# Waiting for the output stores in two steps at the end of SyncE's program

## The chip, the cores and the metric

The kernel runs on one core of one Trainium2 chip. The metric is the device time of an execution in microseconds (us); lower is better. Each kernel was run several times, in rounds that alternate with the kernel before on the same chip. A second number belongs to each execution, the **span**: from the first to the last instruction of the program itself. The timed execution is longer than the span, because closing code runs after the program's last instruction.

A ratio below is the mean time of one kernel's fast runs over that of the other's of the same rounds, so it is not quite the ratio of the medians that are quoted beside it. A run counts as slow when it is more than 1.5% above the fastest of the same kernel; slow runs are left out of the ratios, but not of the medians. Spans of single runs are on record to 0.1 us, so a difference of time and span is good to 0.05 us.

## The reference

For x of 2048 x 448 (bf16), the result is x plus two branches of its layer norm: a linear attention with 16 heads and a softmax feature map, and a dense SiLU block.

```python
xn = _layernorm(x, axis=-1)
return x + _A_ref(xn, A_wqkv, A_w_phi, A_wo) + _B_ref(xn, B_w1, B_w2)
```

Only the way the result leaves the chip matters for what follows: 16 tiles of 128 rows are written from on-chip memory to HBM as they are finished.

## The kernel before

The kernel schedules its own operations and then emits one instruction stream for each engine. A finished tile is added up by VectorE and stored by a DMA. Stores are numbered, and number n counts on the semaphore of slot n mod 4. The last tile is split in two halves: ScalarE issues the first half's store, SyncE the second's.

```python
NOS = 4
out_sems = [sem(f"s_out{i}") for i in range(NOS)]
# ... cut ...
def out_ev(t, ob, addend, cs):
    res = x_sb[:, t, :]
    P.op("dve", ..., lambda e: e.tensor_tensor(res[:, cs], ob, addend[:, cs], ALU.add), ..., name="out_ev")
    P.dma(lambda e: e.dma_start(out=rows_of(out, t, t + 1)[:, 0, cs], in_=res[:, cs]), ..., name="out_dma",
          out_slot=ob_cnt[0] % NOS, eng="sp" if cs.start else "act")
    ob_cnt[0] += 1
```

There are 17 stores, so the slots take 5, 4, 4 and 4 of them. Each store adds 16 to its slot's semaphore. SyncE issues most of the kernel's loads and transpositions as well; its program ends with waits for all slots, so that nothing ends before the output has landed:

```python
def emit_engine(ename, eng):
    waited = {}
    for oid in order[ename]:
        # ... cut: the waits that this operation needs ...
        ins = o.fn(eng)
        if o.is_dma:
            ins.then_inc(o.dma_sem, 16)
        # ... cut ...
    if ename == "sp":
        for i in range(NOS):
            if out_cnt[i] > 0:
                eng.wait_ge(out_sems[i], 16 * out_cnt[i])
```

A wait call is not yet an instruction. In the compiled program two calls share one wait instruction, and they are paired from the inside of the list to the outside. The four calls 0, 1, 2, 3 become two instructions: (slot 2 full, slot 1 full), then (slot 3 full, slot 0 full). The store that lands last is the 17th, on slot 0.

The softmax here doesn't subtract the row's maximum and nothing guards it: scores larger than these inputs give would overflow.

## Time and profile before

| | before |
|---|---|
| time, median of the first 3 runs | 149.02 us (148.81 to 149.06) |
| span of the profiled run | 147.6 us |
| TensorE busy | 143.4 us, 97% |
| SyncE instructions | 79 |
| last compute instruction ends | 145.98 us |
| last store lands | 147.61 us |

The lines that carry the table are shown and read in the prediction. In them, SPq is SyncE's own queue of instructions, L1119 is line 1119 of the kernel, and 28/218/407 are the least, median and greatest duration in ns. One more table: the same kernel cut at the 501st matmul and at the end of TensorE's work. Its columns are stretch and length, then the busy times of TensorE matmul, weight load, VectorE, ScalarE and GpSimd with instruction counts, then clock, DMA share and GB/s.

```profile
0.00:46.60 46.60, 44.45 (x500) 25.72 (x502) 32.78 (x85) 32.58 (x48) 25.10 (x56) 1.00 0.83 199
46.60:145.50 98.90, 98.90 (x1076) 54.03 (x1070) 57.80 (x111) 39.24 (x44) 48.94 (x37) 1.00 0.44 82
145.50:147.70 2.20, 0.04 (x1) 0.00 (x0) 0.47 (x2) 0.00 (x0) 0.00 (x0) 1.00 0.28 80
```

TensorE waits 2 us in all in the first stretch, never in the second, and is done in the third.

### The profile page before, as it was taken

Reading aid. Unit: us, or ns where it says so; the run is one execution under the profiler, and the core shown is the slowest. Engines: PE = TensorE matmul, PEld = TensorE weight load, DVE = VectorE, ACT = ScalarE, POOL = GpSimd, SP = SyncE. Lnnn points to the kernel's source line nnn. Section 1 sums busy time; section 2 is a strip of 40 time slices with the busy share of each in tenths; the row PEclk is TensorE's granted clock in tenths of the full one; section 3 lists DMA queues with packets and bytes.
Section 4 is the critical chain, followed back from the end, with each engine's and each line's share of the span. In section 5 each row is a group of like instructions: output and inputs, shape, how many; then the busy total and the mean of one; then the engine's idle time right before and its main releaser. Section 6 shows DMA issues by size and latency. Waiting matters only on the chain.

```text
span 147.6 us, 3735 instructions
## 1 busy us (share of the span) xinstructions
PE 143.4 (97%) x1572; PEld 79.7 (54%) x1572; DVE 91.1 (62%) x196; ACT 71.8 (49%) x92; POOL 74.0 (50%) x92
## 2 busy tenths in 40 slices
PE   7989999999999999999999999999999999999994
PEld 7884444544544557655444455555555465555473
DVE  2958997190799889207993018969701958252383
ACT  4657675759994988998655597080000000000000
POOL 8618566501099999996999600983940000000000
PEclk9999999999999999999999999999999999999999
DMA  4999964899920000000387391079676925542154
GB/s 109 331 355 247 295 119 70 154 134 301 334 61 0 0 0 4 4 4 0 41 172 147 77 141 36 0 148 119 127 142 134 232 84 98 107 38 39 34 174 137
DMA packets 44496, 17.53 MB, mean 119 GB/s; under 512 B 37040, under 2 KB 44096, under 8 KB 44480
## 3 DMA queue, kind: packets, MB, share of 16 engines
q1 hardware_dynamic: 41648, 15.10, 50.5%
q10 hardware_dynamic: 2704, 2.17, 4.4%
q8 instruction: 12, 0.20, 0.6%
q0 software_dynamic: 128, 0.03, 0.1%
q14 instruction: 4, 0.03, 0.1%
HBM read 6.57 MB, written 1.84 MB: 57 GB/s over the span
## 4 chain that ended last, share of the span: by engine, by line
PE 92%; DMA 4%; SPq 1%; DVE 1%; issue 1%; ACT 0%
PE psum L482 91%; DMA phT<-in_B_w_dram 4%; SPq L516 1%; DVE x_sb L896 1%; DVE Wqk L636 0%; PE psum L497 0%; ACT last_lo L502 0%; ACT last_hi L502 0%
## 5 line engine op out<-in xcount | busy, mean ns | idle before, releaser
L482 PE MATMUL psum<-xnT,phT 64*128 64x512 bf16 (+1 forms) x428 | 45.6, 350 | 0.9 <-DMA phT<-in_B_w_dram 0.4
L482 PE MATMUL psum<-w_sb,hT 128*128 128x448 bf16 (+1 forms) x238 | 45.4, 341 | 0.0
L814 POOL TENSOR_TENSOR RA<-Ek_sb,Rec 128x896 bf16<-128x896 bf16 x16 | 27.0, 1721 | 13.1 <-DVE Rec L779 10.2
L502 ACT ACTIVATE hT<-psum 128x1024 bf16<-128x1024 f32 x28 | 27.3, 1024 | 12.8 <-PE psum L482 12.8
L778 DVE TENSOR_REDUCE Rec<-Ek_sb 128x32 f32<-128x896 bf16 (+1 forms) x20 | 24.4, 1252 | 14.4 <-POOL Ek_sb L509 7.5
L482 PEld LDWEIGHTS psum<-w_sb,hT 128*128 128x128 bf16 x238 | 22.2, 98 | 18.7 <-issue 1.1
L482 PEld LDWEIGHTS psum<-xnT,phT 64*128 64x128 bf16 (+1 forms) x428 | 21.0, 95 | 20.9 <-PE psum L482 0.6
L502 ACT ACTIVATE Ek_sb<-psum 128x864 bf16<-128x864 f32 x24 | 20.1, 910 | 7.1 <-POOL RA L814 4.4
L482 PE MATMUL psum<-Wqk,xnT 64*128 64x432 bf16 x224 | 23.4, 343 | 0.1
L874 DVE TENSOR_SCALAR den<-psum 128x16 f32<-128x16 f32 x16 | 2.3, 156 | 23.3 <-PE psum L482 23.3
L482 PEld LDWEIGHTS psum<-Wqk,xnT 64*128 64x128 bf16 x224 | 10.5, 94 | 10.1 <-issue 0.8
L788 POOL TENSOR_TENSOR Ek_sb<-Ek_sb,Rec 128x896 bf16<-128x896 bf16 x8 | 13.3, 1700 | 5.1 <-DVE Rec L779 5.1
L788 POOL TENSOR_TENSOR phT<-phT,Rec 128x896 bf16<-128x896 bf16 x8 | 13.3, 1702 | 0.0
L482 PE MATMUL psum<-wv,xnT 64*128 64x448 bf16 x112 | 12.9, 349 | 0.0
L643 DVE BATCH_NORM_STATS2 st<-x_sb 128x6 f32<-128x448 bf16 x16 | 9.6, 603 | 2.9 <-DMA x_sb<-in_A_x_dram 2.9
L482 PE MATMUL psum<-wo_sb,vaug 128*128 128x448 bf16 (+1 forms) x51 | 10.8, 342 | 0.0
L896 DVE TENSOR_TENSOR x_sb<-psum,x_sb 128x448 bf16<-128x448 f32 (+1 forms) x14 | 7.5, 584 | 5.0 <-PE psum L482 5.0
L881 DVE TENSOR_TENSOR vaug<-psum,rden 128x448 bf16<-128x448 f32 x16 | 9.8, 623 | 0.4
L658 DVE TENSOR_SCALAR RA<-x_sb,mv,rstd 128x384 bf16<-128x384 bf16 (+4 forms) x29 | 8.9, 346 | 1.3 <-POOL rstd L654 1.1
L779 DVE RECIPROCAL Rec<-Rec 128x32 f32<-128x32 f32 (+1 forms) x24 | 8.8, 396 | 0.2
L778 DVE TENSOR_REDUCE Rec<-phT 128x64 f32<-128x1792 bf16 x4 | 8.0, 2004 | 0.6 <-ACT phT L502 0.6
L482 PEld LDWEIGHTS psum<-wv,xnT 64*128 64x128 bf16 x112 | 5.5, 94 | 5.2
(59 smaller groups left out, 110.6 us busy)
## 6 DMA issues: line engine op xcount, KB each, us to landing
out_dram<-x_sb ACTq DMA_DIRECT2D x15, 112.0 KB, 1.7
w_sb<-in_B_w_dram SPq DMA_DIRECT2D x1, 1568.0 KB, 8.1
x_sb<-in_A_x_dram SPq DMA_DIRECT2D x3, 448.0 KB, 6.2
wo_sb<-in_A_wo_dram SPq DMA_DIRECT2D x2, 336.0 KB, 7.6
phT<-in_B_w_dram SPq DMA_DIRECT2D x1, 576.0 KB, 7.2
phT<-in_B_w_dram SPq DMA_DIRECT2D x2, 256.0 KB, 4.5
phT<-in_B_w_dram ACTq DMA_DIRECT2D x1, 384.0 KB, 4.8
wv<-in_A_wqkv_dram SPq DMA_DIRECT2D x1, 336.0 KB, 7.3
```

Source lines behind the costliest of these rows:

```text
L482: r = e.matmul(dst, lhsT, rhs, start=st, stop=sp, skip_group_check=True)
L502: P.op("act", d_act(n), lambda e: e.activation(dst, src, func, scale=scale), reads=[src], writes=[dst], table=table, name=name, **keys)
L516: P.dma(lambda e: e.dma_start(out=dst, in_=src), n / 280.0, writes=[dst], name=name, eng=eng, lat=lat)
L643: P.op("dve", 590, lambda e: e.bn_stats(st6[:, t, :], xs), reads=[xs], writes=[st6[:, t, :]], name=f"bnst{t}", okeys_w=["ln"])
L658: P.op("dve", dur, lambda e: e.tensor_scalar(dst, x_sb[:, t, c0:c1], mv[:, t, 0:1], rstd[:, t:t + 1], ALU.subtract, ALU.mult), reads=[xs, ...
L778: P.op("dve", 50 + 967 * n, lambda e: e.tensor_reduce(R2, E4, AXL.X, ALU.add), reads=[E4], writes=[R2], name="Ssum")
L779: P.op("dve", 135 + 210 * n, lambda e: e.reciprocal(R2, R2), reads=[R2], writes=[R2], name="Rrec")
L788: P.op("pool", 1700, lambda e: e.tensor_tensor(E3, E3, Rk[:, :, None].broadcast_to([128, 32, DH]), ALU.mult), reads=[E3, Rk], writes=[E3], ...
L814: P.op("pool", 1700, lambda e: e.tensor_tensor(dst, Eq, Rq.rearrange("p (c j) -> p c j", c=CC)[:, :, :, None].broadcast_to([128, CC, 4, DH ...
L874: P.op("dve", 190, lambda e: e.tensor_scalar(den[:, uq, :], U3[:, :, DH], EPS_DEN, None, ALU.add), reads=[U3[:, :, DH]], writes=[den[:, uq ...
L881: P.op("dve", 620, lambda e: e.tensor_tensor(o3, U3[:, :, 0:DH], rden[:, uq, :, None].broadcast_to([128, H, DH]), ALU.mult), reads=[U3[:, ...
L896: P.op("dve", d_dve(cs.stop - cs.start), lambda e: e.tensor_tensor(res[:, cs], ob, addend[:, cs], ALU.add), reads=[ob, addend[:, cs]], wri ...
```

## The change

The intent can be read from the code: SyncE first waits for all stores but the last of each slot, then for the last, so that most of the waiting work is done before the last store lands. The lower counts prove nothing that the full counts do not, so the result is the same.

```diff
             if ename == "sp":
-                for i in range(NOS):
-                    if out_cnt[i] > 0:
-                        eng.wait_ge(out_sems[i], 16 * out_cnt[i])
+                for back in (1, 0):
+                    for i in range(NOS):
+                        if out_cnt[i] > back:
+                            eng.wait_ge(out_sems[i], 16 * (out_cnt[i] - back))
```

Eight calls in place of four make four wait instructions in place of two. The rest of every engine's program is unchanged.

## The prediction

> **What bounds the kernel now.** I read the page first, then the stretch table of the end, the chain, the timeline of the last microseconds, and last the one source line that the change touches.
>
> ```profile
> span 147.6 us, 3735 instructions
> PE 143.4 (97%) x1572; PEld 79.7 (54%) x1572; DVE 91.1 (62%) x196; ACT 71.8 (49%) x92; POOL 74.0 (50%) x92
> q14 instruction: 4, 0.03, 0.1%
> PE 92%; DMA 4%; SPq 1%; DVE 1%; issue 1%; ACT 0%
> ```
>
> TensorE is busy for 97% of the span and makes up 92% of the chain that ended last. SyncE does not appear among the engines of the first part: its program only issues transfers and waits. So nothing that SyncE does in the first 146 us matters unless it delays a transfer that TensorE needs, and the change leaves that part of its program alone. The third line counts instruction packets on one queue; it is used further down.
>
> The stretch table shows where TensorE stops:
>
> ```profile
> 140.00:146.00 6.00, 5.54 (x48) 4.08 (x46) 4.54 (x9) 0.00 (x0) 0.00 (x0) 1.00 0.50 172
> 146.00:147.70 1.70, 0.00 (x0) 0.00 (x0) 0.00 (x0) 0.00 (x0) 0.00 (x0) 1.00 0.25 68
> ```
>
> The columns after the length are the busy times of TensorE matmul, weight load, VectorE, ScalarE and GpSimd, with instruction counts, then clock, DMA share and GB/s. From 146.0 us on, no compute engine does anything. The last 1.6 us are a store and a wait. The timeline and the view of the store and of the waiting line say what happens in them:
>
> ```profile
> 145.20 0.78 DVE L896 TENSOR_TENSOR x_sb<-psum,x_sb 128x224 bf16<-128x224 f32 x2 [0.76 <-PE psum L482]
> 145.62 0.34 ACTq L898 DMA_DIRECT2D out_dram<-x_sb  x1
> 146.07 0.37 SPq L898 DMA_DIRECT2D out_dram<-x_sb  x1
> ```
> ```profile
> L1119 SPq EVENT_SEMAPHORE  x2: 28/218/407, 146.5 to 147.2; - x2
> ```
> ```profile
> SPq L1119 <- DMA out_dram<-x_sb: 1.1, 1, 1.1
> ```
> ```profile
> out_dram<-x_sb SPq DMA_DIRECT2D x1, 56.0 KB, 1.5
> ```
>
> VectorE ends the two half tiles at 145.20 + 0.78 = 145.98. ScalarE issues the first half's store at 145.62, SyncE the second half's at 146.07 and is free at 146.44. Then SyncE runs the waiting line, L1119. The source has four wait calls there, one for each output slot, but the row says x2: two wait instructions, so two semaphores go into each. Their durations are 28 and 407 ns (least and most) and they start at 146.5 and 147.2. The second therefore ends at 147.2 + 0.41 = 147.6, the end of the span. The SyncE wait view puts 1.1 us on a landing store, and the issue table has the last store landing 1.5 us after 146.07, at 147.6. So **the landing of the last store ends the program**, and the number of waits in front of it does not show.
>
> **Exact times from the trace's semaphore records**, since the views round. Slots 1 and 2 reached their full counts at 145.65 and 146.16, before the first wait instruction ran (146.48). Slot 3 (the ScalarE half) was full at 147.210; the last wait instruction is recorded from 147.226. Slot 0 (the SyncE half) was full at 147.611; that instruction ends at 147.633. Of the 407 ns, some 385 are the wait for slot 0.
>
> **What the Trainium skill says.**
> "Perfetto Trace Analysis", section "Sequencer-only Instruction (DRAIN, etc)": the reported start of such an instruction comes when all its semaphores are satisfied, so waiting is not in its duration. This trace agrees for the first semaphore (start 16 ns after slot 3 was full) and differs for the second, whose 385 ns are inside the 407.
> "DMA: Bandwidth & Descriptors", section "Why a DMA increments its semaphore by 16 and not by 1": only a full count proves that a transfer landed; a lower count with two transfers in flight can be filled by either. The added waits use a lower count, so they prove nothing, but the full-count waits stay behind them and keep the program right. The trace has exactly 16 landing records for each store.
> "Runtime: NRT & Kernel Launch", section "Instruction fetch mechanics": instructions are fetched in blocks of 16 KiB, 256 instructions, ahead of use, and crossing a block is "mostly hidden". The trace has 12 packets of 16 KiB on queue 8, as that says, but queue 14's are 8 KiB each (0.03 MB over 4), which would be 128 instructions. No run here shows yet whether a crossing costs SyncE anything.
>
> **The change, part by part.** Stores go round four slots; there are 15 + 1 on ScalarE and 1 on SyncE, 17, so the slots hold 5, 4, 4 and 4. The new first pass waits for all but the last of each slot: counts 64, 48, 48, 48. That is four more wait calls, which at two to an instruction are **two more instructions**. Nothing is removed or moved; the old four calls stay last.
>
> What the new ones wait for: by the semaphore records, slot 0 had its 64 at 145.09, slot 1 its 48 at 142.75, slot 2 at 143.26, slot 3 at 144.56. SyncE gets to them at 146.48. The youngest is 1.39 us old, so neither waits. Each then costs what a satisfied two-semaphore wait costs: 28 ns busy, and 58 to 65 ns from start to start of the next instruction where SyncE runs one directly ahead of another instruction (at 75.03, 90.55 and 124.48 us). Two cost 2 x 0.06 = 0.12 us.
>
> What that lies beside: the first old wait instruction is done at 146.51 and the second can't pass its first semaphore before 147.21, so there are 0.70 us of slack. 0.12 of 0.70 is used. On the path to the end: **0.00 us**. The span should stay at 147.6. If the time follows the span, the prediction is 149.02.
>
> **The rivals.**
> (1) *A later last wait.* If the pairing changes so that slot 0's full count is no longer in the last instruction, the others run after it landed: one to three satisfied instructions of 0.06 us, +0.06 to +0.17 us. For it: the compiler already reorders (it paired slots 2 and 1, then 3 and 0). Against: the pair with slot 0 was put last before. Time: up to 149.2.
> (2) *The instruction fetch.* The timed 149.02 is 1.4 us more than the span, so something after the last wait is in it. In the trace's packet records, an 8 KiB instruction packet of queue 14 starts at 148.72, 1.09 us after the last wait. SyncE's own store at 146.07 had its first packet at 146.93, 0.86 us later, and its first load, issued at 0.80, at 1.84, 1.04 us later. So a fetch that starts at 148.72 may have been asked for at about 147.7 to 147.9, just after SyncE's last instruction. It is plausibly SyncE's: VectorE accounts for two of the four inside the span (22.5 and 122.2 us, when it had started 61 and 189 instructions, 128 apart), and ScalarE and GpSimd can hold the two at 41.2 and 44.0. If two more instructions move SyncE's block boundary to the near side of its wait, the request falls into time that is waited out anyway. What it then saves is at most the packet's 0.46 us, and some of that may have been beside the closing work of other engines: -0.1 to -0.4, 148.6 to 148.9. For it: the position. Against: the skill calls the crossing mostly hidden, and nothing in this trace shows an engine stalled by it.
> (3) *The fetch gets in the way.* The same shift puts an 8 KiB packet near the final store. A packet asked for at 146.55 would start at about 147.5, after the store's last data packet (147.26). Little is at risk: at most a part of 0.46 us on one of 16 engines, 149.0 to 149.4.
>
> **Range and chances.** I give the null 60%, rival 2 30% at about -0.25, the other two 10% at about +0.15. The weighted shift is -0.075 + 0.015 = -0.06 us; I set 148.95. Repeats of the kernel before spread from 148.81 to 149.06. Eight times in ten it should be within 148.55 to 149.25: the lower end is most of rival 2, the upper is rival 1 or a slow repeat. A change of 2% would be 2.98 us, more than the whole 1.6 us from the last compute to the end, and no part of this change touches the TensorE chain. So 0.98 for within 2%, and 0.01 on either side for an unforeseen effect.
>
> **What would show it.** The waiting line should list four instructions, three of about 28 ns and one of some 400, from 146.5 to 147.2, and the span should stay at 147.6 within 0.3. SyncE's wait for the last store should stay at about 1.0 us. If rival 1 holds, the longest of them is not the last and the span grows by 0.06 to 0.17. If rival 2 holds, the span is unchanged, the time falls, and the page counts a fifth packet on queue 14 because it now starts before the span ends. The prediction is wrong if TensorE's busy time or the timeline before 146 us differs by more than repeats do: then the program's length acts on something that no view here shows.

## The result, and the profile after

| | before | after |
|---|---|---|
| time, median of 6 runs | 149.14 us (148.81 to 149.31) | 149.42 us (149.23 to 149.94) |
| ratio, 95% interval | 1 | 1.0025 (1.0005 to 1.0045) |
| span of the profiled run | 147.6 us | 148.0 us |
| timed less span, every run with a span | 1.73 to 1.85 us | 1.23 to 1.30 us |

By the 2% rule this is the same time. It lies above the predicted range all the same, and the last two rows say that something real happened: the span of the profiled run went up, and the time outside the span went down by 0.5 us in every run.

The page of the changed kernel differs in its first line only by what was added, and TensorE's work is what it was:

```profile
span 148.0 us, 3737 instructions
PE 143.1 (97%) x1572; PEld 79.9 (54%) x1572; DVE 91.0 (61%) x196; ACT 71.6 (48%) x92; POOL 74.0 (50%) x92
q14 instruction: 4, 0.03, 0.1%
```

The stretch table of the changed kernel, cut at the same instructions as the one before:

```profile
0.00:46.30 46.30, 44.18 (x500) 25.79 (x502) 32.69 (x85) 32.33 (x48) 25.09 (x56) 1.00 0.83 200
46.30:145.20 98.90, 98.90 (x1076) 54.07 (x1070) 57.82 (x111) 39.23 (x44) 48.94 (x37) 1.00 0.43 82
145.20:148.00 2.80, 0.04 (x1) 0.00 (x0) 0.47 (x2) 0.00 (x0) 0.00 (x0) 1.00 0.21 62
```

The middle stretch has the same length and the same 1076 matmuls. The first is 0.3 us shorter in this execution, which is chance, as shown below. The last is longer by 0.6 us. Its timeline and its waiting line, which was L1119 and is L1120 now:

```profile
144.89 0.77 DVE L896 TENSOR_TENSOR x_sb<-psum,x_sb 128x224 bf16<-128x224 f32 x2 [0.76 <-PE psum L482]
145.76 0.37 SPq L898 DMA_DIRECT2D out_dram<-x_sb  x1
```
```profile
L1120 SPq EVENT_SEMAPHORE  x4: 28/28/28, 147.3 to 148.0; - x4
```
```profile
out_dram<-x_sb SPq DMA_DIRECT2D x1, 56.0 KB, 1.5
```

SyncE is free at 145.76 + 0.37 = 146.13, and its store lands 1.5 us after issue, at 147.3, as before. The four wait instructions were expected to start from 146.1 on. **All four start at 147.3 or later**, each takes 28 ns, and the last starts at 148.0: nothing was waited out ahead of the landing. The trace's records give the exact order (the slots are from the trace, the counts from the compiled program):

| start, us | waits for (compiled program) | |
|---|---|---|
| 147.319 | slot 0 full (80), slot 3 at 48 | slot 0 became full at 147.303 |
| 147.389 | slot 1 full, slot 2 at 48 | |
| 147.877 | slot 2 full, slot 1 at 48 | 0.46 us after the one ahead of it ended |
| 147.956 | slot 3 full, slot 0 at 64 | |

So two things stand out. The call for the last landing, fifth in the list of eight, was paired with the fourth and came **first**. And between the second and third instruction SyncE pauses for 0.46 us, where the others follow each other in 0.07 to 0.08 us from start to start. In the kernel before the pause isn't in the span. But its closing code started late: its barrier's first record after the landing came 0.685 us after the landing, of which only 0.02 were the end of the last wait instruction. In the changed kernel that record came 0.811 us after the landing. The clear difference of the tails is thus 0.126 us, in two parts of opposite sign.

An instruction packet of 8 KiB on queue 14 starts 1.091 us after the end of SyncE's 79th instruction in both traces (at 148.724 and 148.508 us). In the kernel before the 79th instruction is the last wait; in the changed one it is the second of the four.

### The profile page after: what moved, and what is told of

The parts are those of the page before. It is cut to its first block, busy times and chain, and to the rows that moved or that the text cites. A ratio compares the mean times of both kernels' runs of the same rounds, so it can differ in the third digit from the quotient of the medians.

```text
span 148.0 us, 3737 instructions
## 1 busy us (share of the span) xinstructions
PE 143.1 (97%) x1572; PEld 79.9 (54%) x1572; DVE 91.0 (61%) x196; ACT 71.6 (48%) x92; POOL 74.0 (50%) x92
## 4 chain that ended last, share of the span: by engine, by line
PE 90%; DMA 3%; ACT 2%; DVE 1%; SPq 1%; issue 0%
PE psum L482 90%; DMA phT<-in_B_w_dram 3%; ACT hT L502 1%; SPq L516 1%; DVE Wqk L636 1%; DVE x_sb L896 1%; PE psum L497 0%; ACT last_hi L502 0%; ACT last_lo L502 0%
```

## The experiments

Two theories and a null were set against each other. **Theory O** (order and crossing): SyncE pauses for some 0.45 to 0.55 us after its 79th instruction, where it goes into the next block of its program, and each satisfied instruction behind the one that waits for the last landing adds 0.06 us. **Theory L** (length): a longer program is slower, or, turned round, any longer program is free of the pause. **Theory N**: chance.

Three measures are used: the clock with its ratio, the timed execution less span (in each run), and the tail, from the last landing to the first record of the closing barrier after it, in the one trace of each kernel.

### The changed kernel again

No edit.

> The changed kernel once more, for a narrower interval and a second trace. Theory O (order and block crossing: the last-landing store's wait stands first of four, and SyncE stalls some 0.4 to 0.5 us after its 79th instruction, in the old kernel after its last wait, here between the second and third of the four): first wait of the line starts about 0.02 us after the last landing, a gap of about 0.4 to 0.5 us between second and third start, instruction packet about 1.09 us after the second one's end; from last landing to the first record of the closing barrier about 0.81 us against 0.69 before; time +0.10 to +0.20 us against before. Theory L (two more instructions cost by themselves, wherever they stand): +0.1 to +0.4. Theory N (no real difference, spread of the runs): ratio within 0.999 to 1.001.

Median 149.31 us against 149.02, ratio 1.0022 (1.0001 to 1.0042). Tail 0.811 us, the pause 0.460 us, the packet 1.088 us after the 79th instruction's end. Both the order and the pause repeat to a few ns. The ratio alone can't tell 0.1 from 0.6 us.

### Four instructions more, away from the end

```diff
+                if ename == "sp" and order["sp"].index(oid) == 35:
+                    for _ in range(8):
+                        eng.wait_ge(ops[order["sp"][0]].dma_sem, 16)   # landed long ago
                 ins = o.fn(eng)
```

> Before with eight waits that are long met, four instructions, ahead of SyncE's transposition of 71.6 us, where it idles anyway; the four last waits are as before. Theory O: the crossing moves to about 136.5 us, where SyncE idles; from the last landing to the closing barrier about 0.15 us in place of 0.69; time 0.40 to 0.55 us less than before (ratio about 0.997). Theory L: four instructions more, +0.2 to +0.8. Theory N: within 0.1 us of before.

The place named there was wrong: the added waits stood ahead of the third such transposition, at about 75 us, not the first. The same holds for after_pad8, pad_2 and pad_256 below. Median 148.70 us, ratio 0.9981 (0.9956 to 1.0006): the direction is right, but it is 0.32 us less than before where 0.40 to 0.55 was expected, and the interval still contains 1. The other two measures are clear. Timed less span was 1.22 to 1.28 us in all six runs, and the tail 0.144 us against 0.685. **The pause is worth 0.54 us at the end of the kernel before, and it is gone from there** when the 79th instruction is another one. The page counts the packet, too, which now falls inside the span, five in place of four:

```profile
q14 instruction: 5, 0.04, 0.1%
```

The waiting line of this kernel reads as in the kernel before, so the end of the program proper has not changed:

```profile
L1122 SPq EVENT_SEMAPHORE  x2: 28/211/394, 146.3 to 147.0; - x2
```

### The changed kernel with the same four instructions

> The changed kernel with the same four instructions ahead of the transposition of 71.6 us. Theory O: no stall at the end any more, only the order: three satisfied instructions of 0.06 us follow the one that waits for the last landing, so 0.18 us more than pad_8 and 0.2 to 0.4 us less than before; landing to barrier about 0.33 us. Theory L: six instructions more, the slowest of all. Theory N: within 0.1 us of before.

Median 148.83 us, ratio 0.9982 (0.9964 to 1.0000). Tail 0.365 us, 0.221 more than the kernel above. This is the cost of the order, with the pause out of the way:

```profile
L1123 SPq EVENT_SEMAPHORE  x4: 28/28/28, 147.4 to 147.6; - x4
```

Four starts within 0.2 us (147.429, 147.498, 147.560, 147.624), all behind the landing at 147.413: three instructions of 0.065 us, and the first ends 0.02 us later behind the landing than the last wait of pad_8 did. Theory L had this one, the longest so far, as the slowest of all; it is faster than the changed kernel.

### The changed kernel's length with the right order

The exact undoing of the order, the same eight calls with slot 0 full in the last pair, was refused by the race check ahead of a run: slot 3's count of 48 can be reached by either of two sets of stores in flight, so such a wait in front proves nothing. The repeats below are for full counts instead, against the kernel before:

```diff
-                for i in range(NOS):
-                    if out_cnt[i] > 0:
-                        eng.wait_ge(out_sems[i], 16 * out_cnt[i])
+                for i, back in ((0, 0), (1, 0), (2, 0), (1, 0), (2, 0), (1, 0), (2, 0), (3, 0)):
+                    eng.wait_ge(out_sems[i], 16 * (out_cnt[i] - back))
```

> As long as the changed kernel (81 SyncE instructions, four wait instructions at the end), but every wait for a full count, slots 1 and 2 asked three times, and the pair with slots 3 and 0 last. Theory O: the crossing after the 79th instruction falls between the second and third wait instruction at about 146.6 us, ahead of the landing, and is waited out: 0.40 to 0.55 us less than before, same as pad_8, and 0.5 to 0.7 us less than the changed kernel. Theory L: as slow as the changed kernel. Theory N: within 0.1 us of before.

Median 148.74 us, ratio 0.9985 (0.9962 to 1.0009): by the clock 0.28 us less than before, where 0.40 to 0.55 was expected. Tail 0.148 us, timed less span 1.19 to 1.32 us.

```profile
L1118 SPq EVENT_SEMAPHORE  x4: 28/28/407, 146.6 to 147.3; - x4
```

This is what the prediction had drawn for the change: four instructions from 146.6 on, three of 28 ns, and the last at 147.3 with 407 ns. The pause is there (0.453 us between the second and the third) but it is waited out anyway. So with 81 instructions, the order decides between a tail of 0.81 and one of 0.15 us.

### The kernel before against itself

> The kernel before, run against itself: the noise of a ratio here. All theories: ratio 1.000; its interval shows what a difference of 0.3 us is worth. The timed execution less the span is 1.74 to 1.82 us in every run, as in the 11 runs of before in the first experiment; last landing to closing barrier as in the first trace.

Median 149.40 us against 149.19, ratio 1.0031 (0.9997 to 1.0064). The interval contains 1, but the middle is further from 1 than the changed kernel's. One run of 151.0 us was counted as fast. So **a ratio of 1.002 or 1.003 is not evidence here**. Timed less span was 1.78 to 1.82 us, the tail 0.679 us: these measures repeat to 0.04 and 0.01 us.

### The order alone, at the old length

```diff
-                for i in range(NOS):
-                    if out_cnt[i] > 0:
-                        eng.wait_ge(out_sems[i], 16 * out_cnt[i])
+                for i, back in ((1, 0), (0, 0), (3, 0), (2, 0)):
+                    eng.wait_ge(out_sems[i], 16 * (out_cnt[i] - back))
```

> Before with its four wait calls in the order 1, 0, 3, 2: still 79 instructions, but the pair with the two last landings (slots 3 and 0) is now first and the long-met pair last. Theory O: one satisfied instruction follows the landing, and the stall still follows the last: from last landing to barrier 0.05 to 0.08 us more than before, timed execution less span still 1.8 us, time +0.06 us, which the clock can't show. Rival (the order costs nothing, it is all the length): tail unchanged to 0.02 us.

Tail 0.750 us, 0.07 more than before, and timed less span still 1.75 to 1.81 us; median 149.53 us, ratio 1.0018 (1.0004 to 1.0031). One satisfied instruction behind the landing costs one instruction:

```profile
L1118 SPq EVENT_SEMAPHORE  x2: 28/218/408, 147.3 to 147.8; - x2
```

The same two durations as in the kernel before, but the long one is now the one at 147.3 and the short one follows.

### One instruction more

As pad_8 with range(2): 80 instructions.

> Before with one instruction more ahead of the transposition of 71.6 us: 80 instructions. Theory O: the crossing comes between the two last wait instructions, about 0.1 us after the first, and is waited out: timed execution less span 1.25 us, tail from last landing to barrier 0.54 us shorter than before, time 0.3 to 0.55 us less. Rival: if the boundary is not exactly after the 79th instruction but one later, the stall stays after the last wait and nothing changes (1.8 us).

Median 148.82 us over all six runs; a sixth run, of 151.44 us, was slow, and without it the median is 148.78 us and the ratio 0.9966 (0.9953 to 0.9979). Tail 0.172 us, timed less span 1.24 to 1.33 us. A single instruction, far from the end, takes 0.5 us off the tail. With the pause seen between the 79th and 80th in the changed kernel and in full81, this puts the boundary exactly behind the 79th instruction.

### A block of 128 instructions more

As pad_8 with range(256): 207 instructions.

> Before with 256 long-met waits, 128 instructions, ahead of the transposition of 71.6 us: the SyncE program is 207 instructions long. Theory O (a block of 128 instructions, and a stall where SyncE goes into the next one): the first crossing falls among the added waits, while SyncE idles, and the second is again right after the last wait, so the stall at the end is back: timed execution less span 1.8 us (1.25 in the four kernels of the first experiment), an instruction packet about 1.09 us after the last wait, same time as before. Rival P (any longer program is free of the stall): 1.25 us, 0.5 us less than before.

Median 154.84 us; two of the six runs were slow, and without them the median is 154.45 us and the ratio 1.0336 (1.0294 to 1.0378). **This missed the expected time**: 128 instructions of 0.06 us stood where SyncE isn't idle, and held up a transposition from 75.1 to 83.4 us, and with it TensorE. The tail is still of use: 0.578 us, timed less span 1.64 to 1.73 us, and a packet 1.005 us after the last wait. The pause came back. Inside the added waits, the one behind the 79th instruction started 0.447 us after that ended.

### The same, in SyncE's idle time

```diff
-                if ename == "sp" and order["sp"].index(oid) == 35:
+                if ename == "sp" and order["sp"].index(oid) == 33:
```

> Again 128 instructions more (207), but really in SyncE's idle time: in the earlier run they stood ahead of the third transposition (75.1 us) and held it up for 8.5 us. Here they stand ahead of the first one, where SyncE has been idle since 36.6 us. Theory O (blocks of 128): nothing is held up, the first crossing is among the added ones, the second again after the last wait: timed execution less span 1.65 to 1.8 us, time within 0.3 us of before. Rival P (any longer program is free of the stall at the end): 1.25 us and 0.5 us less than before.

Median 149.12 us, ratio 0.9988 (0.9962 to 1.0014): the time is back at that of the kernel before. Tail 0.578 us, timed less span 1.65 to 1.74 us, a packet 0.995 us after the last wait, and a pause of 0.456 us behind the 79th instruction, at 39.3 us, where it costs nothing. Among the added waits, numbers 36 to 163, no other step from one start to the next takes even 0.1 us. The **block is 128 instructions**: position 79 and position 207 behave alike. Rival P, that any longer program is free of the pause, is out.

### One instruction more, in SyncE's idle time

As pad_2 with number 33.

> One instruction more (80), ahead of the first transposition of 71.6 us: the smallest version that should beat both kernels. Theory O: as pad_2: timed execution less span 1.25 us, last landing to barrier about 0.2 us, ratio to before about 0.9965. Theory N: ratio 1.000.

Median 148.62 us against 149.21, ratio 0.9956 (0.9932 to 0.9979); tail 0.171 us, timed less span 1.25 to 1.29 us. It is faster than the kernel before by 0.51 us by the tail and 0.59 us by the medians, or 0.4%: the interval is clear of 1, and the gain well under 2%. It was not run in the same rounds as the changed kernel; its tail is 0.64 us shorter than that one's.

### One instruction fewer

```diff
-        NOS = 4
+        NOS = 2
```

> Two output slots in place of four: the last waits shrink to one instruction, 78 in all. Theory O: the crossing after the 79th instruction comes one instruction after the program's own last wait, in the closing code, so the stall stays: timed execution less span 1.8 us, same time as before to 0.1 us. Rival S (a shorter program is a faster one): 0.06 us less, or with the stall gone 0.5 us less.

Median 149.01 us, ratio 0.9998 (0.9968 to 1.0027). Tail 0.572 us, timed less span 1.66 to 1.69 us where 1.8 was expected. The pause stays, in the closing code, but the tail is 0.11 us shorter than before where one instruction of 0.06 us would have been at most expected. That the pause is 0.43 us in this kernel and the two with 207 instructions, and 0.54 us in the kernel before, is not explained.

### All tails side by side

| kernel | SyncE instructions | 79th (or 207th) is | last landing to closing barrier, us | timed less span, us |
|---|---|---|---|---|
| before, twice | 79 | last wait | 0.685, 0.679 | 1.73 to 1.85 |
| order79 | 79 | last wait | 0.750 | 1.75 to 1.81 |
| after, twice | 81 | second of 4 waits, behind the landing | 0.811, 0.811 | 1.20 to 1.30 |
| full81 | 81 | second of 4 waits, ahead of the landing | 0.148 | 1.19 to 1.32 |
| pad_2, pad_2_idle | 80 | first wait, ahead of the landing | 0.172, 0.171 | 1.24 to 1.33 |
| pad_8 | 83 | a transposition at 135 us | 0.144 | 1.22 to 1.28 |
| after_pad8 | 85 | a transposition at 135 us | 0.365 | 1.20 to 1.25 |
| pad_256, pad_256_idle | 207 | last wait | 0.578, 0.578 | 1.64 to 1.74 |
| short78 | 78 | first instruction of the closing code, by count | 0.572 | 1.66 to 1.69 |

Where does the rest of the spread come from? In the traces the start of TensorE's 501st matmul varies from 45.89 to 46.83 us. From there to the start of the last matmul it is 98.64 to 98.69 us in every trace but that of the kernel that held up a transposition, and from there to the last landing 2.31 to 2.33 us. So what differs from trace to trace, apart from the tail, lies in the first 47 us, before anything that the change could touch.

The clock can be held against the tails as well. In the rounds of after_again, pad_8, after_pad8, full81, before_again, order79 and pad_2, the median, less that of the kernel before, lay 0.13 to 0.28 us above the difference of the tails. The kernel before against itself is among them, with 0.21 us. In the rounds of pad_256_idle, pad_2_idle and short78 it lay between 0.09 us below and 0.02 us above. Since the unchanged kernel shows it as well, an excess of this size is no evidence for an edit; where it comes from is not known.

## Why the prediction was wrong

**What bounds the kernel: right.** TensorE's stretch and the landing of the last store are the same in both traces.

**The count, right; the order, wrong.** Two instructions were added, as said. But the prediction took the new waits to run first and the old ones to "stay last". The step that failed is its own objection to rival 1: "the pair with slot 0 was put last before". The pairing folds the list, so the fifth call of eight lands in the first pair. The prediction knew that the compiler had paired slots 2 and 1, then 3 and 0; the fold of a list is a rule that gives these pairs, and could have been tried on eight calls.

**"On the path to the end: 0.00 us": wrong.** The 0.70 us of slack was real, as full81 shows, but the first instruction waited through it, so nothing was put into it. Three instructions came behind the landing. Rival 1 had sized this at up to 0.17 us; the runs show 0.221 us for it alone (after_pad8 against pad_8).

**The null's link from span to time: wrong.** The prediction kept the span and let the time follow. The span of the profiled run rose by 0.4 us, and the time outside it fell by about 0.5 us in every run, because the pause moved from behind the last instruction to between two of them. The 1.4 us that the prediction saw outside the span were misread, too: they are the median of some executions less the span of another one. The profiled run itself took 149.45 us for its span of 147.6.

**Rival 2, the block crossing: right in kind, without effect in sum.** It had 30% and at most 0.46 us. The crossing is SyncE's, it was right behind the last wait, and it costs 0.54 us there (pad_8). Two instructions did move it to the near side of the program's last wait, but not ahead of the landing, because of the order. In the changed kernel it still costs 0.811 - 0.365 = 0.446 us. So the sum is + 0.221 for the order and 0.446 - 0.541 = - 0.095 for the pause: **+ 0.126 us**. What the prediction priced as two separate rivals with different signs were one event. Its mechanism for the cost is only half shown: the pause ends 0.63 us before the packet of 8 KiB starts (147.877 against 148.508), so SyncE is not waiting for that packet. Nor does the packet keep its distance: in full81, pad_2 and pad_2_idle it starts 1.36 to 1.41 us after the end of the 79th instruction. What SyncE does in the pause, no view shows.

**Rival 3, a packet in the way of the store: no sign of it.** The last store landed 1.54 us after its issue began both times (147.611 - 146.066 and 147.303 - 145.759). There the packet came after the landing; in full81 and pad_2, whose 79th instruction ends ahead of the landing, the store took 1.54 and 1.55 us as well.

**The range: too low.** The changed kernel's median lies 0.40 us above the 149.02 that the prediction started from. Of these, 0.12 are the kernel before itself, whose median over six runs was 149.14, and 0.13 are the tail. The rest, 0.15, is not shown to come from the change: the kernel before against itself gave 0.21. With 148.95 as the centre, below the time before, the upper end of 149.25 left little room for the case that rival 1 came with rival 2's gain lost.

## What to carry to other kernels

Read the order of the last waits from the compiled program, not from the source: the wait for the event that comes last belongs in the last instruction, and whatever stands behind it is paid in full. A short engine program that ends near a block boundary can pay a pause of half a microsecond behind its last wait; compare the timed execution with the span, and if a kernel of this kind is to be squeezed, place one harmless instruction in an idle stretch rather than at the end. Where the effect is under 0.3%, measure the stretch that the change touches in the trace, and run the old kernel against itself before believing a ratio.

## What the Trainium skill lacked or had wrong

- "Runtime: NRT & Kernel Launch", section "Instruction fetch mechanics", gives blocks of 256 instructions (16 KiB). On SyncE the runs show 128: the pause comes behind instruction 79 and again behind 207, with packets of 8 KiB on queue 14. The 12 packets of queue 8 are 16 KiB, as the page says; by count they are TensorE's (3174 instructions are 12.4 blocks of 256). Whether this machine was set to another block size for SyncE is not on record.
- The same section calls a crossing "mostly hidden". On SyncE the runs show a pause of 0.45 to 0.46 us between two waits at a crossing, and 0.43 to 0.54 us at the end of the program, where nothing hides it. The page has no number for it.
- "Perfetto Trace Analysis", section "Sequencer-only Instruction (DRAIN, etc)", says of instructions that the sequencer alone carries out, with DRAIN as the example, that the reported time starts when all semaphores are satisfied. For SyncE's wait instruction on two semaphores the runs show the start 16 ns after one was satisfied and the wait for the other inside the duration (407 ns against 28).
- No page of those read says in which order wait calls are paired into instructions. Here four calls gave (third, second), (fourth, first), and eight gave (fifth, fourth) to (eighth, first); the order with the last landing first cost 0.221 us.
